# A channel MLP's head: three token tiles transposed raw and multiplied in cells of 386 columns, instead of two in cells of 258

## The chip, the cores and the metric

One core of one Trainium2 chip. The metric is the device time of one execution in microseconds; 398.56 us is the median of three runs of the kernel before (398.45 to 398.8).

## The reference

```python
def _gelu(x):
    return jax.nn.gelu(x, approximate=True)

def _layernorm(x, axis=-1, eps=1e-5):
    m = jnp.mean(x, axis=axis, keepdims=True)
    v = jnp.var(x, axis=axis, keepdims=True)
    return (x - m) / jnp.sqrt(v + eps)

def reference(x, w1, b1, w2, b2):
    y = _layernorm(x, axis=-1)
    h = _gelu(jnp.einsum("bsd,df->bsf", y, w1) + b1)
    return jnp.einsum("bsf,fd->bsd", h, w2) + b2
```

x is 1 x 2048 x 1024, w1 1024 x 3584, w2 3584 x 1024, all bf16; x and the biases are normal times 0.05.

## The kernel before, in words

**Tiling.** The 2048 tokens are 16 tiles of 128, four tiles to a block of 512 columns. D = 1024 is eight depth tiles, F = 3584 is 28 rows of 128. For each block the first product fills 28 PSUM rows of 512 columns (`pe_row`, line 386: eight matmuls of 512 columns, one for each depth tile), ScalarE puts each through Gelu with b1 into `hT_sb` (`act_gelu`, line 409), and the second product (`out_chunk`, line 451) makes eight groups of 28 matmuls from `hT_sb` and w2. VectorE adds b2 and SP stores. Both products want the tokens on the free axis, so x is transposed into `yT_sb`. For blocks 1 to 3 VectorE does the layernorm and the transposes (lines 255 to 269 and 312) under TensorE's work. PE works through one list in a fixed order; each engine has such a list, and they meet in semaphores.

**The head.** Block 0 can't wait for all of that. SP's queue loads x tile 0, x tile 1, four w1 chunks, x tile 2, four more chunks, x tile 3 (`SP_FIRST_LOADS`), then the wide w1 chunks, block 1, w2, b2 and the rest. A chunk of the first eight is two depth tiles of 512 columns: 256 KB in rows of 1 KB. PE runs 27 spin matmuls (`warm`), then transposes tiles 0 and 1 raw, not normalised (`pe_T`, line 342), into four PSUM banks; ScalarE copies them to `yT_sb` (line 358). Then comes the wave: seven rows (`R`), one in each of seven PSUM banks. For each row and depth tile a cell of 258 columns (`pe_wave`, line 399) multiplies both raw tiles and two columns of ones; the ones give the sum over depth of w1, which a raw tile needs for its mean. Tile 2 is normalised by VectorE (`ops_norm`), transposed after cell 50, and multiplied in 56 cells of 128 columns; then tile 3 the same way, transposed at cell 36 of tile 2's pass. Both pass through the bank `ps_t`.

**Making up for raw.** The statistics of the raw tiles are turned into rows (`ops_row_turn`, line 484) and spread over the partitions by ScalarE (`put_row_spread`, line 490). For each of the seven rows VectorE then adds minus the mean times the column sum (line 518) and multiplies by the reciprocal deviation (line 521): the fix, before that row's Gelu. The 21 later rows of block 0 are full rows of 512 columns. For them the raw tiles are centred in place in `yT_sb` (`ops_centre`, line 511, one subtraction per tile, allowed when the raw cells are done), and only the multiplication by the reciprocal deviation is left (line 425).

**Order around it.** VectorE's list in the head is: statistics of tiles 0 and 1, b1's transposes (line 496) and its cast (line 499), the turn, statistics and normalisation of tiles 2 and 3, centring, seven fixes. After it `crit` (scalings, b2 additions) and `fill` (layernorm and transposes of the next block) are merged by estimated due times, from `T_PE_START`, `T_DVE_START`, `est` and the cost that each entry carries. `new_unit` deals out PSUM banks: the seven of the wave, then the five of `ps_1` in a ring; a row waits for the Gelu that last read its bank. `SLOT_0` puts block 0's raw tiles at columns 128 to 383 of `yT_sb`, tile 2 at 384, tile 3 at 0.

Of the kernel before, what the change touches and what calls it, by code (L numbers as in the profile page):

```python
# [20 lines left out]
RAW = (0, 1)  # L21
# [5 lines left out]
ROWS = ((0, 1, 2, 3), (4, 5, 6))  # L27
QUARTERS = (0, 2, 4, 6, 8)
T2_AT = 50
T3_AT = 36  # L30
W1_EARLY = 2
W1_EARLY_COLS = 512
W1_COLS = (512, 1024, 1024)
N_W2_CHUNKS = 4
SP_FIRST_LOADS = ("x0", "x1", "w0", "w1", "w2", "w3", "x2", "w4", "w5", "w6", "w7", "x3")
ACT_FIRST_LOADS = ("b1",)
SLOT_0 = (1, 2, 3, 0)
N_ONES = 2

T_PE_START = 5.8  # L40
T_DVE_START = 21.0
# [54 lines left out]
def bass_standalone__mixer_channel_mlp__prompt_kernel(  # L96
# [25 lines left out]
    assert TPB == 4 and RAW == (0, 1) and sum(ROWS, ()) == tuple(range(R))  # L122

    w1_chunks = [(j0, j1, k * W1_EARLY_COLS, (k + 1) * W1_EARLY_COLS) for k in range(W1_EARLY)
                 for j0, j1 in zip(QUARTERS[:-1], QUARTERS[1:])]
# [21 lines left out]
    with ExitStack() as es:  # L147
# [6 lines left out]
        yT_sb = sb("yT_sb", [P, 2, DT, TB], BF16)  # L154
# [3 lines left out]
        b1r_sb = sb("b1r_sb", [32, P], BF16)  # L158
        b1t_sb = sb("b1t_sb", [P, 32], BF16)
# [3 lines left out]
        stat_r = sb("stat_r", [P, 2, 4], F32)  # L163
        row_r = sb("row_r", [P, 4, P], F32)
# [9 lines left out]
        ps_2 = ps("ps_2", [P, NB2, 512], F32)  # L174
        ps_1b = ps_1[:, :, :].bitcast(BF16)
# [39 lines left out]
        def issue(item):  # L215
            if item == "b1":
                dma(b1r_sb[0:FT, :], b1.rearrange("(t p) -> t p", p=P), "b1", F * 2, waits=["b1z"])
            elif item[0] == "x":
                load_x_tile(int(item[1:]))
            elif item[0] == "w" and int(item[1:]) < len(w1_chunks):  # L220
                load_w1(int(item[1:]))
# [22 lines left out]
        pool.op(lambda e: e.memset(b1r_sb[:, :], 0.0), sig="b1z")  # L244
        one0 = SLOT_0[0] * P - N_ONES
        pool.op(lambda e: e.memset(yT_sb[:, 0, :, one0:one0 + N_ONES], 1.0), sig="onecols")
# [54 lines left out]
        def ops_T(i):  # L301
            blk, t = divmod(i, TPB)
            waits = [y_ev[i][-1]]
            if blk - 2 in mm1_done:
                waits.append(mm1_done[blk - 2])
            res = []
            for tq in range(4):
                for q in range(4):
                    src = x_sb[32 * tq:32 * (tq + 1), i, :].rearrange("p (j q a) -> p j q a", j=DT, q=4)[:, :, q, :]
                    dst = yT_sb[32 * q:32 * (q + 1), blk % 2, :, t * P + 32 * tq:t * P + 32 * (tq + 1)]  # L310
                    lastop = (tq == 3 and q == 3)
                    res.append((lambda e, src=src, dst=dst: e.transpose(out=dst, in_=src),  # L312
                                waits, (f"tr{i}" if lastop else None), 0.47))
            yT_ev[i] = [f"tr{i}"] * DT
            return res
# [6 lines left out]
        bank_of = {"t": ps_t[:, 0, :], "2_0": ps_2b[:, 0, :], "2_1": ps_2b[:, 1, :], "1_4": ps_1b[:, 4, :]}  # L322
        slot = lambda i: SLOT_0[i] if i < TPB else i % TPB

        def pe_T(i, groups, banks):
            blk = i // TPB
            t = slot(i)
# [21 lines left out]
            for k, (g0, g1) in enumerate(zip(groups[:-1], groups[1:])):  # L349
                bname = banks[k]  # L350
                if bname != prev:
                    off = 0
                prev = bname
                done = max(m for m in range(len(banks)) if banks[m] == bname)
                src = bank_of[bname][:, off:off + (g1 - g0) * P].bitcast(I32)
                src = src.rearrange("p (j s) -> p j s", j=g1 - g0)
                dst = yT_sb[:, blk % 2, g0:g1, t * P:(t + 1) * P].bitcast(I32)
                act.op(lambda e, dst=dst, src=src: e.copy(out=dst, in_=src), waits=[f"tp{i}_{done}"],  # L358
                       sig=f"te{i}_{k}")
                off += (g1 - g0) * P  # L360
                bank_read[bname] = f"te{i}_{k}"
# [5 lines left out]

        def new_unit():
            u = unit_n[0]
            unit_n[0] += 1  # L370
            bank = first_ring[u] if u < len(first_ring) else ("1", (u - len(first_ring)) % NB1)
            waits = [bank_gelu[bank]] if bank in bank_gelu else []
            name = f"{bank[0]}_{bank[1]}"
            if not waits and name in bank_read:
                waits.append(bank_read[name])
            return bank, waits

        def unit_bank(bank):
            return (ps_1 if bank[0] == "1" else ps_2)[:, bank[1], :]

        def pe_row(b, r, bank, waits, sig):
            for dt in range(DT):
                w = list(waits) if dt == 0 else []
                w += [f"w1c{w1_chunk_of(r, dt)}"]
                w += [yT_ev[b * TPB + t][dt] for t in range(TPB)]
                pe.op(lambda e, b=b, r=r, dt=dt, bank=bank: e.matmul(  # L386
                    unit_bank(bank)[:, 0:TB], lhsT=w1_sb[:, dt, r * P:(r + 1) * P], rhs=yT_sb[:, b % 2, dt, :],
                    start=(dt == 0), stop=(dt == DT - 1)),
                    waits=w, sig=(sig if dt == DT - 1 else None))
            pe_t[0] += DT * _mm_us(TB)  # L390
            est[sig] = pe_t[0]

        def pe_wave(r, dt, tiles, bank, waits, sig):
            n0 = slot(tiles[0]) * P - (N_ONES if tiles[0] == 0 else 0)
            n1 = (slot(tiles[-1]) + 1) * P
            w = list(waits) + [f"w1c{w1_chunk_of(r, dt)}"] + [yT_ev[t][dt] for t in tiles]
            if tiles[0] == 0:
                w.append("onecols")
            pe.op(lambda e: e.matmul(  # L399
                unit_bank(bank)[:, n0:n1], lhsT=w1_sb[:, dt, r * P:(r + 1) * P], rhs=yT_sb[:, 0, dt, n0:n1],  # L400
                start=(dt == 0 and tiles[0] in (0, 3)), stop=(dt == DT - 1), skip_group_check=True),
# [15 lines left out]
        def mm1_row(b, r):  # L417
# [4 lines left out]
            if b == 0:  # L422
                reg = raw_cols(bank)
                ready = f"sc_{r}"
                crit.append((est[sig], (lambda e, reg=reg: e.tensor_tensor(out=reg, in0=reg, in1=row_b(1), op=ALU.mult),  # L425
                                        [sig, "row_r"], ready, 0.45), 0))
# [10 lines left out]
        def out_chunk(b, st, c0, c1, region, prev_store):  # L437
# [11 lines left out]
            for ft in range(FT):  # L449
                sl = slot(b * TPB + st)  # L450
# [28 lines left out]
        def ops_row_turn():  # L479
            res = []  # L480
            for tq in range(4):
                src = flat[32 * tq:32 * (tq + 1), :, :].to_broadcast([32, 4, 32])
                dst = row_r[0:32, :, 32 * tq:32 * (tq + 1)]
                res.append((lambda e, src=src, dst=dst: e.transpose(out=dst, in_=src), ["rstd0", "rstd1"],  # L484
                            ("row_q" if tq == 3 else None), 0.31))
# [7 lines left out]
        def ops_b1():  # L493
            res = []
            for q in range(4):
                res.append((lambda e, q=q: e.transpose(out=b1t_sb[32 * q:32 * (q + 1), :],
                                                       in_=b1r_sb[:, 32 * q:32 * (q + 1)]),
                            ["b1", "b1z"], ("b1t" if q == 3 else None), 0.2))
            res.append((lambda e: e.tensor_copy(out=b1_sb[:, :], in_=b1t_sb[:, 0:FT]), ["b1t"], "b1c", 0.18))
            return res  # L500

        row_b = lambda k: row_r[:, :, :].rearrange("p (t k) s -> p t k s", k=2)[:, :, k, :]
        raw_cols = lambda bank: unit_bank(bank)[:, slot(0) * P:(slot(1) + 1) * P].rearrange("p (t s) -> p t s", t=2)
        bank_col = lambda bank: bank[1] + (0 if bank[0] == "1" else NB1)

        def ops_centre():
            res = []
            for t in RAW:
                xt = yT_sb[:, 0, :, slot(t) * P:(slot(t) + 1) * P]
                m = row_r[:, 2 * t, :].unsqueeze(1).to_broadcast([P, DT, P])  # L510
                res.append((lambda e, xt=xt, m=m: e.tensor_tensor(out=xt, in0=xt, in1=m, op=ALU.subtract),  # L511
                            ["row_r", "wave01"], f"ctr{t}", 1.23))
# [23 lines left out]
        pe_T(1, GROUPS_0, ("2_1", "1_4"))  # L536
        put_row_spread()
# [9 lines left out]
        cells = [(r, dt) for rows in ROWS for j0, j1 in zip(QUARTERS[:-1], QUARTERS[1:])  # L547
                 for r in rows for dt in range(j0, j1)]
        for n, (r, dt) in enumerate(cells):
            if n == T2_AT:  # L550
                pe_T(2, GROUPS_1, ("t",))
            wave_cell(r, dt, RAW, "wave01" if n == len(cells) - 1 else None)
        n = 0
        for j0, j1 in zip(HALVES[:-1], HALVES[1:]):
            for r in range(R):
                for dt in range(j0, j1):
                    if n == T3_AT:
                        pe_T(3, GROUPS_1, ("t",))
                    n += 1
                    wave_cell(r, dt, (2,), f"w2_{r}" if dt == DT - 1 else None)  # L560
        cs_ev = {}
        for c0, c1, src in ((0, NB1, ps_1[:, 0:NB1, one0:one0 + 1]), (NB1, R, ps_2[:, 0:NB2, one0:one0 + 1])):
            mine = [r for r in range(R) if c0 <= bank_col(wave[r][0]) < c1]
            act.op(lambda e, c0=c0, c1=c1, src=src: e.mul(ncs[:, c0:c1].unsqueeze(2), src, -1.0),
                   waits=[f"w2_{mine[-1]}"], sig=f"cs{c0}")
            for r in mine:
                cs_ev[r] = f"cs{c0}"
        for r in range(R):
# [3 lines left out]
            for o in ops_fix(r, wave[r][0]):  # L572
# [3 lines left out]
        for t in RAW:  # L576
            yT_ev[t] = [f"ctr{t}"] * DT
# [93 lines left out]
```

## Time and profile before

| | |
|---|---|
| median of three runs | 398.56 us |
| the profiled execution | 398.81 us |
| its span | 397.6 us |
| PE busy | 391.5 us (98%) |
| full rows, line 386: one matmul | 379 ns, 821 recorded |
| second product, line 451: one matmul | 379 ns (128 x 512), 964 recorded with the narrow ones |
| PE, waits for w1 in the head (matmul rows) | 1.4 us |
| VectorE, DVE transposes, line 312 | 83.7 us, 192 of them |
| w1 chunks of 256 KB: from issue to landing | 5.5 us (median of 8) |

A matmul's duration holds the depth of the array, so it is longer than the distance from one to the next; its end is modelled. Some matmul records are missing. "PEld" is the loading of weights, "SPq" SP's issuing of DMAs; a bracket gives the idle time of the engine before the group and what ended it. Idle time of an engine that is not on the path costs nothing.

### The profile page before, as it was taken

The numbers are of one execution on the slowest core, as the hardware profiler recorded it, in microseconds if no ns is written. First come the engines' busy times: TensorE is split into PE (matmuls) and PEld (weight loads), VectorE is DVE, ScalarE is ACT, GpSimd is POOL, SyncE is SP. The second block draws the span as 40 slices with busy tenths as digits, with TensorE's granted clock in tenths as the row PEclk, the third lists the DMA queues.
The fourth block names the chain that finished last, engine by engine and source line by source line (L and its number), as shares of the span: only waits on it lengthen the run. The fifth ranks groups of instructions, "written<-read, shape, count | busy, mean of one in ns | idle before, by whom it ended". The sixth has DMA issues, their size and how long they took to land.

```text
span 397.6 us, 4718 instructions
## 1 busy us (share of the span) xinstructions
PE 391.5 (98%) x2015; PEld 189.7 (48%) x2050; DVE 154.3 (39%) x335; ACT 82.7 (21%) x124; POOL 10.6 (3%) x56
## 2 busy tenths in 40 slices
PE   8999999999999999999999999999999999999998
PEld 7844444444444444444444444444444444444446
DVE  5759898989999005988100000001100000001111
ACT  3264430000134432000024433100003334400000
POOL 2101000020001000000000000000000000000000
DMA  7999930000000000000000000000000000000001
GB/s 252 375 387 387 387 145 15 26 26 16 26 1 2 0 0 2 26 14 28 26 15 0 0 2 0 12 16 26 13 28 13 2 0 0 2 13 26 15 26 28
DMA packets 16350, 23.64 MB, mean 59 GB/s; under 512 B 1482, under 2 KB 8522, under 8 KB 16330
## 3 DMA queue, kind: packets, MB, share of 16 engines
q1 hardware_dynamic: 16288, 23.33, 16.7%
q8 instruction: 16, 0.26, 0.3%
q14 instruction: 4, 0.03, 0.0%
q10 hardware_dynamic: 42, 0.01, 0.0%
HBM read 19.14 MB, written 4.19 MB: 59 GB/s over the span
## 4 chain that ended last, share of the span: by engine, by line
PE 95%; DMA 2%; SPq 1%; issue 1%; DVE 1%; POOL 0%
PE ps L451 48%; PE ps L386 45%; DMA x_sb<-in_x_dram 2%; SPq L192 1%; PE ps L399 1%; DVE st_sb L255 0%; PE ps_t L342 0%; POOL rstd_sb L262 0%; DVE x_sb L269 0%; DVE o_sb L462 0%; DVE mv_sb L265 0%
## 5 line engine op out<-in xcount | busy, mean ns | idle before, releaser
L451 PE MATMUL ps<-w_sb,hT_sb 128*128 128x512 bf16 (+1 forms) x964 | 193.4, 360 | 0.8
L386 PE MATMUL ps<-yT_sb,w_sb 128*128 128x512 bf16 x821 | 180.8, 379 | 1.0
L451 PEld LDWEIGHTS ps<-w_sb,hT_sb 128*128 128x128 bf16 x980 | 91.3, 98 | 102.6
L409 ACT ACTIVATE hT_sb<-ps,b_sb 128x512 bf16<-128x512 f32 x112 | 76.8, 688 | 253.2 <-PE ps L386 231.8
L386 PEld LDWEIGHTS ps<-yT_sb,w_sb 128*128 128x128 bf16 x840 | 82.1, 98 | 98.9
L462 DVE TENSOR_TENSOR o_sb<-ps,b_sb 128x512 bf16<-128x512 f32 (+1 forms) x35 | 22.6, 646 | 198.9 <-PE ps L451 198.9
L312 DVE STREAM_TRANSPOSE yT_sb<-x_sb 32x256 bf16<-32x256 bf16 x192 | 83.7, 436 | 26.4 <-PE ps L386 23.3
L255 DVE BATCH_NORM_STATS2 st_sb<-x_sb 128x6 f32<-128x512 bf16 x32 | 20.9, 671 | 7.3 <-DMA x_sb<-in_x_dram 7.3
L399 PE MATMUL ps<-yT_sb,w_sb 128*128 128x128 bf16 (+1 forms) x168 | 13.4, 237 | 1.4 <-DMA w_sb<-in_w_dram 1.4
L399 PEld LDWEIGHTS ps<-yT_sb,w_sb 128*128 128x128 bf16 x168 | 11.4, 98 | 3.1 <-DMA w_sb<-in_w_dram 2.2
L262 POOL TENSOR_TENSOR rstd_sb<-mv_sb,nhalf 128x1 f32<-128x1 f32 x14 | 7.7, 549 | 115.0 <-DVE mv_sb L265 115.0
L425 DVE TENSOR_TENSOR ps<-ps,row_r 128x256 f32<-128x256 f32 x21 | 8.9, 427 | 4.7 <-PE ps L386 4.7
L269 DVE TENSOR_SCALAR x_sb<-x_sb,mv_sb,rstd_sb 128x1024 bf16<-128x1024 bf16 x14 | 7.6, 544 | 3.3 <-POOL rstd_sb L262 2.7
L473 PE MATMUL ps<-const-bfloat16-1.0 128*128 128x128 bf16 x30 | 3.4, 300 | 0.8 <-PEq L656 0.8
L473 PEld LDWEIGHTS ps<-const-bfloat16-1.0 128*128 128x128 bf16 x30 | 3.0, 139 | 0.8 <-issue 0.8
L518 DVE SCALAR_TENSOR_TENSOR ps<-row_r,ncs,ps 128x256 f32<-128x256 f32 x7 | 3.4, 480 | 0.0
L265 DVE BATCH_NORM_AGGREGATE mv_sb<-st_sb 128x2 f32<-128x15 f32 x14 | 3.1, 222 | 0.4
L358 ACT COPY yT_sb<-ps_t 128x512 int32<-128x512 int32 (+1 forms) x3 | 1.5, 516 | 7.7 <-PE ps_t L342 7.7
L521 DVE TENSOR_TENSOR ps<-ps,row_r 128x256 f32<-128x256 f32 x7 | 3.0, 432 | 0.2
L490 ACT COPY row_r<-row_r 32x512 f32<-32x512 f32 x3 | 1.9, 617 | 3.2 <-DVE row_r L484 3.2
L511 DVE TENSOR_TENSOR yT_sb<-yT_sb,row_r 128x1024 bf16<-128x1024 bf16 x2 | 2.4, 1216 | 0.0
L342 PE MATMUL ps_t<-ident,x_sb 128*128 128x128 bf16 x20 | 1.7, 226 | 0.1
(21 smaller groups left out, 12.5 us busy)
## 6 DMA issues: line engine op xcount, KB each, us to landing
w_sb<-in_w_dram SPq DMA_DIRECT2D x4, 1792.0 KB, 18.3
w_sb<-in_w_dram SPq DMA_DIRECT2D x2, 2048.0 KB, 15.9
out_dram<-o_sb SPq DMA_DIRECT2D x31, 128.0 KB, 1.7
x_sb<-in_x_dram SPq DMA_DIRECT2D x3, 1024.0 KB, 14.3
w_sb<-in_w_dram SPq DMA_DIRECT2D x8, 256.0 KB, 5.5
x_sb<-in_x_dram SPq DMA_DIRECT2D x4, 256.0 KB, 4.2
w_sb<-in_w_dram SPq DMA_DIRECT2D x1, 1024.0 KB, 9.0
b_sb<-in_b_dram SPq DMA_DIRECT2D x1, 256.0 KB, 14.3
```

The source lines that it names most:

```text
L192: dma_q[0].op(lambda e, dst=dst, src=src: e.dma_start(dst, src), waits=waits, sig=sig, sem="d_" + sig, inc=16)
L255: return (lambda e, i=i, h=h, pw=pw: e.bn_stats(st_sb[i][:, 6 * h:6 * (h + 1)], x_sb[:, i, h * pw:(h + 1) * pw]), [x_ev[i][h if len(x_ev[i ...
L262: pool.op(lambda e, i=i, dst=dst, mv=mv: e.tensor_tensor(out=dst, in0=mv[:, 1:2], in1=nhalf[:, i:i + 1], op=ALU.pow), waits=[f"mv{i}", "nh ...
L269: return (lambda e, i=i, c0=c0, c1=c1: e.tensor_scalar(out=x_sb[:, i, c0:c1], in0=x_sb[:, i, c0:c1], scalar1=mv_sb[:, i, 0:1], scalar2=rst ...
L312: res.append((lambda e, src=src, dst=dst: e.transpose(out=dst, in_=src), waits, (f"tr{i}" if lastop else None), 0.47))
L386: pe.op(lambda e, b=b, r=r, dt=dt, bank=bank: e.matmul(unit_bank(bank)[:, 0:TB], lhsT=w1_sb[:, dt, r * P:(r + 1) * P], rhs=yT_sb[:, b % 2, ...
L399: pe.op(lambda e: e.matmul(unit_bank(bank)[:, n0:n1], lhsT=w1_sb[:, dt, r * P:(r + 1) * P], rhs=yT_sb[:, 0, dt, n0:n1], start=(dt == 0 and ...
L409: act.op(lambda e, r=r, n0=n0, n1=n1, bank=bank: e.activation(out=hT_sb[:, r, n0:n1], in_=unit_bank(bank)[:, n0:n1], func=ACT.Gelu_apprx_tanh,
L425: crit.append((est[sig], (lambda e, reg=reg: e.tensor_tensor(out=reg, in0=reg, in1=row_b(1), op=ALU.mult), [sig, "row_r"], ready, 0.45), 0))
L451: pe.op(lambda e, sl=sl, ft=ft, c0=c0, c1=c1, bank=bank: e.matmul(ps_2[:, bank, 0:c1 - c0], lhsT=hT_sb[:, ft, sl * P:(sl + 1) * P], rhs=w2 ...
L462: crit.append((est[sig], (lambda e, ob=ob, c0=c0, c1=c1, bank=bank: e.tensor_tensor(out=o_sb[:, ob, c0:c1], in0=ps_2[:, bank, 0:c1 - c0], ...
L473: pe.op(lambda e: e.matmul(ps_1[:, 0, 0:P], lhsT=ones, rhs=ones, start=True, stop=True))
```

## The change

It loads tile 2 third and transposes it raw like tiles 0 and 1, so that a cell has 386 columns (three tiles and the two columns of ones) and the pass for tile 2 is gone; only tile 3 is normalised first and has a pass of 56 cells, transposed at cell 42 of the raw cells. The first eight w1 chunks are four depth tiles of 256 columns (rows of 512 bytes), and the cells go by pairs of rows. b1 is transposed on PE into `ps_t`, between tiles 1 and 2, and copied by ScalarE; its zero fill and VectorE's five instructions for it go. `yT_sb` has two columns more: the ones are at 0 and 1, every tile starts two columns later, and full rows read from column 2. In the first seven rows the raw tiles stand at columns 128 to 511 of the bank and tile 3 at 0; in the later rows tiles stand in order, so `out_chunk` picks its columns of `hT_sb` by row. Turn and spread carry six rows, the fixes and scalings 384 columns. Centring is four subtractions, each over two depth tiles of three token tiles, two before row 0's fix and two behind it. The transposes' bank joins the ring of PSUM banks, ahead of the five of `ps_1`.

```diff
--- before.py
+++ after.py
...
-RAW = (0, 1)
+RAW = (0, 1, 2)
...
-ROWS = ((0, 1, 2, 3), (4, 5, 6))
-QUARTERS = (0, 2, 4, 6, 8)
-T2_AT = 50
-T3_AT = 36
-W1_EARLY = 2
-W1_EARLY_COLS = 512
+ROWS = ((0, 1), (2, 3), (4, 5), (6,))
+CENTRE = (0, 2, 4, 6, 8)
+T3_AT = 42
+W1_EARLY = 4
+W1_EARLY_COLS = 256
...
-SP_FIRST_LOADS = ("x0", "x1", "w0", "w1", "w2", "w3", "x2", "w4", "w5", "w6", "w7", "x3")
+SP_FIRST_LOADS = ("x0", "x1", "x2", "w0", "w1", "w2", "w3", "x3", "w4", "w5", "w6", "w7")
...
-SLOT_0 = (1, 2, 3, 0)
...
-T_PE_START = 5.8
-T_DVE_START = 21.0
+T_PE_START = 5.0
+T_DVE_START = 27.0
...
-                 for j0, j1 in zip(QUARTERS[:-1], QUARTERS[1:])]
+                 for j0, j1 in zip(HALVES[:-1], HALVES[1:])]
...
-        yT_sb = sb("yT_sb", [P, 2, DT, TB], BF16)
+        yT_sb = sb("yT_sb", [P, 2, DT, N_ONES + TB], BF16)
...
-        b1r_sb = sb("b1r_sb", [32, P], BF16)
-        b1t_sb = sb("b1t_sb", [P, 32], BF16)
+        b1r_sb = sb("b1r_sb", [FT, P], BF16)
...
-        stat_r = sb("stat_r", [P, 2, 4], F32)
-        row_r = sb("row_r", [P, 4, P], F32)
+        stat_r = sb("stat_r", [P, len(RAW), 4], F32)
+        row_r = sb("row_r", [P, 2 * len(RAW), P], F32)
...
         def issue(item):
...
-                dma(b1r_sb[0:FT, :], b1.rearrange("(t p) -> t p", p=P), "b1", F * 2, waits=["b1z"])
+                dma(b1r_sb[:, :], b1.rearrange("(t p) -> t p", p=P), "b1", F * 2)
...
-        pool.op(lambda e: e.memset(b1r_sb[:, :], 0.0), sig="b1z")
-        one0 = SLOT_0[0] * P - N_ONES
-        pool.op(lambda e: e.memset(yT_sb[:, 0, :, one0:one0 + N_ONES], 1.0), sig="onecols")
+        pool.op(lambda e: e.memset(yT_sb[:, 0, :, 0:N_ONES], 1.0), sig="onecols")
...
-        bank_of = {"t": ps_t[:, 0, :], "2_0": ps_2b[:, 0, :], "2_1": ps_2b[:, 1, :], "1_4": ps_1b[:, 4, :]}
-        slot = lambda i: SLOT_0[i] if i < TPB else i % TPB
+        bank_of = {"t": ps_t[:, 0, :], "2_0": ps_2b[:, 0, :], "2_1": ps_2b[:, 1, :], "1_2": ps_1b[:, 2, :], "1_3": ps_1b[:, 3, :],
+                   "1_4": ps_1b[:, 4, :]}
+        ycol = lambda i: N_ONES + (i % TPB) * P
+        raw_at = TB - len(RAW) * P
+        one0 = raw_at - N_ONES
...
         def pe_T(i, groups, banks):
...
-            t = slot(i)
...
+        ring = [("t", 0)] + [("1", k) for k in range(NB1)]
+
         def new_unit():
...
-            bank = first_ring[u] if u < len(first_ring) else ("1", (u - len(first_ring)) % NB1)
+            bank = first_ring[u] if u < len(first_ring) else ring[(u - len(first_ring)) % len(ring)]
...
-            name = f"{bank[0]}_{bank[1]}"
+            name = "t" if bank[0] == "t" else f"{bank[0]}_{bank[1]}"
...
         def unit_bank(bank):
-            return (ps_1 if bank[0] == "1" else ps_2)[:, bank[1], :]
+            return ps_tf if bank[0] == "t" else (ps_1 if bank[0] == "1" else ps_2)[:, bank[1], :]
...
         def pe_row(b, r, bank, waits, sig):
...
-                    unit_bank(bank)[:, 0:TB], lhsT=w1_sb[:, dt, r * P:(r + 1) * P], rhs=yT_sb[:, b % 2, dt, :],
+                    unit_bank(bank)[:, 0:TB], lhsT=w1_sb[:, dt, r * P:(r + 1) * P], rhs=yT_sb[:, b % 2, dt, ycol(0):ycol(0) + TB],
...
         def pe_wave(r, dt, tiles, bank, waits, sig):
-            n0 = slot(tiles[0]) * P - (N_ONES if tiles[0] == 0 else 0)
-            n1 = (slot(tiles[-1]) + 1) * P
+            raw = tiles == RAW
+            n0, n1 = (one0, TB) if raw else (0, raw_at)
+            y0 = 0 if raw else ycol(tiles[0])
...
-            if tiles[0] == 0:
+            if raw:
...
-                unit_bank(bank)[:, n0:n1], lhsT=w1_sb[:, dt, r * P:(r + 1) * P], rhs=yT_sb[:, 0, dt, n0:n1],
-                start=(dt == 0 and tiles[0] in (0, 3)), stop=(dt == DT - 1), skip_group_check=True),
+                unit_bank(bank)[:, n0:n1], lhsT=w1_sb[:, dt, r * P:(r + 1) * P], rhs=yT_sb[:, 0, dt, y0:y0 + n1 - n0],
+                start=(dt == 0), stop=(dt == DT - 1), skip_group_check=True),
...
-                reg = raw_cols(bank)
+                reg = raw_cols(bank, 0)
...
-                                        [sig, "row_r"], ready, 0.45), 0))
+                                        [sig, "row_r"], ready, 0.57), 0))
...
-                sl = slot(b * TPB + st)
+                sl = (st + raw_at // P) % TPB if b == 0 and ft < R else st
...
         def ops_row_turn():
...
-                src = flat[32 * tq:32 * (tq + 1), :, :].to_broadcast([32, 4, 32])
+                src = flat[32 * tq:32 * (tq + 1), :, :].to_broadcast([32, 2 * len(RAW), 32])
...
-                res.append((lambda e, src=src, dst=dst: e.transpose(out=dst, in_=src), ["rstd0", "rstd1"],
-                            ("row_q" if tq == 3 else None), 0.31))
+                res.append((lambda e, src=src, dst=dst: e.transpose(out=dst, in_=src), [f"rstd{t}" for t in RAW],
+                            ("row_q" if tq == 3 else None), 0.38))
...
         def put_row_spread():
...
-        def ops_b1():
-            res = []
-            for q in range(4):
-                res.append((lambda e, q=q: e.transpose(out=b1t_sb[32 * q:32 * (q + 1), :],
-                                                       in_=b1r_sb[:, 32 * q:32 * (q + 1)]),
-                            ["b1", "b1z"], ("b1t" if q == 3 else None), 0.2))
-            res.append((lambda e: e.tensor_copy(out=b1_sb[:, :], in_=b1t_sb[:, 0:FT]), ["b1t"], "b1c", 0.18))
-            return res
+        def pe_b1():
+            pe.op(lambda e: e.transpose(out=ps_t[:, 0, 0:FT], in_=b1r_sb[:, :], identity=ident[0:FT, 0:FT]),
+                  waits=["ident", "b1", bank_read["t"]], sig="b1t")
+
+        def put_b1():
+            act.op(lambda e: e.copy(out=b1_sb[:, :], in_=ps_t[:, 0, 0:FT]), waits=["b1t"], sig="b1c")
+            bank_read["t"] = "b1c"
...
-        raw_cols = lambda bank: unit_bank(bank)[:, slot(0) * P:(slot(1) + 1) * P].rearrange("p (t s) -> p t s", t=2)
+        raw_cols = lambda bank, c0: unit_bank(bank)[:, c0:c0 + len(RAW) * P].rearrange("p (t s) -> p t s", t=len(RAW))
...
         def ops_centre():
...
-            for t in RAW:
-                xt = yT_sb[:, 0, :, slot(t) * P:(slot(t) + 1) * P]
-                m = row_r[:, 2 * t, :].unsqueeze(1).to_broadcast([P, DT, P])
+            for k, (j0, j1) in enumerate(zip(CENTRE[:-1], CENTRE[1:])):
+                xt = yT_sb[:, 0, j0:j1, ycol(RAW[0]):ycol(RAW[0]) + len(RAW) * P]
+                xt = xt.rearrange("p j (t s) -> p j t s", t=len(RAW))
+                m = row_b(0).unsqueeze(1).to_broadcast([P, j1 - j0, len(RAW), P])
...
-                            ["row_r", "wave01"], f"ctr{t}", 1.23))
+                            ["row_r", f"raw_{R - 1}"], f"ctr{k}", 0.83))
...
         def ops_fix(r, bank):
...
-            reg = raw_cols(bank)
+            reg = raw_cols(bank, raw_at)
...
-        nm = {i: ops_norm(i) for i in (2, 3)}
+        nm = {3: ops_norm(3)}
...
-        seq = st[0][:2] + st[1][:2] + [st[0][2], st[1][2]] + ops_b1() + turn
-        for i in (2, 3):
-            seq += st[i] + nm[i]
-        seq += ctr
+        seq = st[0] + st[1] + st[2] + turn + st[3] + nm[3] + ctr[:2]
...
+        pe_b1()
+        pe_T(2, GROUPS_0, ("1_3", "1_2"))
+        put_b1()
...
-        cells = [(r, dt) for rows in ROWS for j0, j1 in zip(QUARTERS[:-1], QUARTERS[1:])
+        cells = [(r, dt) for rows in ROWS for j0, j1 in zip(HALVES[:-1], HALVES[1:])
...
-            if n == T2_AT:
-                pe_T(2, GROUPS_1, ("t",))
-            wave_cell(r, dt, RAW, "wave01" if n == len(cells) - 1 else None)
-        n = 0
-        for j0, j1 in zip(HALVES[:-1], HALVES[1:]):
-            for r in range(R):
-                for dt in range(j0, j1):
-                    if n == T3_AT:
-                        pe_T(3, GROUPS_1, ("t",))
-                    n += 1
-                    wave_cell(r, dt, (2,), f"w2_{r}" if dt == DT - 1 else None)
+            if n == T3_AT:
+                pe_T(3, GROUPS_1, ("t",))
+            wave_cell(r, dt, RAW, f"raw_{r}" if dt == DT - 1 else None)
...
-                   waits=[f"w2_{mine[-1]}"], sig=f"cs{c0}")
+                   waits=[f"raw_{mine[-1]}"], sig=f"cs{c0}")
...
-            for o in ops_fix(r, wave[r][0]):
+            for o in ops_fix(r, wave[r][0]) + (ctr[2:] if r == 0 else []):
...
-            yT_ev[t] = [f"ctr{t}"] * DT
+            yT_ev[t] = [f"ctr{k}" for k, (j0, j1) in enumerate(zip(CENTRE[:-1], CENTRE[1:])) for _ in range(j0, j1)]
...
```

More of the change, by code (lines that the diff above doesn't have):

```diff
@@ L121, in bass_standalone__mixer_channel_mlp__prompt_kernel @@
     assert all(c[-1] == DT for c in (GROUPS_0, GROUPS_1, HALVES))
-    assert TPB == 4 and RAW == (0, 1) and sum(ROWS, ()) == tuple(range(R))
+    assert TPB == 4 and RAW == (0, 1, 2) and sum(ROWS, ()) == tuple(range(R))
     w1_chunks = [(j0, j1, k * W1_EARLY_COLS, (k + 1) * W1_EARLY_COLS) for k in range(W1_EARLY)
-                 for j0, j1 in zip(QUARTERS[:-1], QUARTERS[1:])]
+                 for j0, j1 in zip(HALVES[:-1], HALVES[1:])]
     c0 = W1_EARLY * W1_EARLY_COLS
@@ L174, in bass_standalone__mixer_channel_mlp__prompt_kernel @@
         ps_2 = ps("ps_2", [P, NB2, 512], F32)
+        ps_tf = ps_t[:, 0, :].bitcast(F32)
         ps_1b = ps_1[:, :, :].bitcast(BF16)
@@ L309, in ops_T @@
                     src = x_sb[32 * tq:32 * (tq + 1), i, :].rearrange("p (j q a) -> p j q a", j=DT, q=4)[:, :, q, :]
-                    dst = yT_sb[32 * q:32 * (q + 1), blk % 2, :, t * P + 32 * tq:t * P + 32 * (tq + 1)]
+                    dst = yT_sb[32 * q:32 * (q + 1), blk % 2, :, ycol(i) + 32 * tq:ycol(i) + 32 * (tq + 1)]
                     lastop = (tq == 3 and q == 3)
@@ L356, in pe_T @@
                 src = src.rearrange("p (j s) -> p j s", j=g1 - g0)
-                dst = yT_sb[:, blk % 2, g0:g1, t * P:(t + 1) * P].bitcast(I32)
+                dst = yT_sb[:, blk % 2, g0:g1, ycol(i):ycol(i) + P].bitcast(I32)
                 act.op(lambda e, dst=dst, src=src: e.copy(out=dst, in_=src), waits=[f"tp{i}_{done}"],
```

## The prediction

> **What bounds the kernel now.** I read the page's engine totals and chain of waits first, then the time line of PE and the windows of the head, then the groups by form. The chain belongs to PE almost from end to end:
>
> ```profile
> PE 391.5 (98%) x2015; PEld 189.7 (48%) x2050; DVE 154.3 (39%) x335; ACT 82.7 (21%) x124; POOL 10.6 (3%) x56
> PE 95%; DMA 2%; SPq 1%; issue 1%; DVE 1%; POOL 0%
> ```
>
> So only what moves PE's first full row (line 386, row 7) moves the end: from there PE runs without a gap (49 matmuls in 10.74 us, over and over in the chain). The head of PE's time line (start, length, group):
>
> ```profile
> 4.75 0.34 PE L473 MATMUL ps<-const-bfloat16-1.0 128*128 128x128 bf16 x3
> 6.21 3.69 PE L399 MATMUL ps<-yT_sb,w_sb 128*128 128x258 bf16 x32 [1.13 <-DMA w_sb<-in_w_dram]
> 10.16 2.34 PE L399 MATMUL ps<-yT_sb,w_sb 128*128 128x258 bf16 x18 [0.26 <-DMA w_sb<-in_w_dram]
> 12.34 0.61 PE L342 MATMUL ps_t<-ident,x_sb 128*128 128x128 bf16 x8
> 12.79 3.02 PE L399 MATMUL ps<-yT_sb,w_sb 128*128 128x258 bf16 x42
> 15.90 0.62 PE L342 MATMUL ps_t<-ident,x_sb 128*128 128x128 bf16 x8
> 16.36 4.41 PE L399 MATMUL ps<-yT_sb,w_sb 128*128 128x128 bf16 x76
> ```
>
> Durations there hold a pipeline's depth, so I take pitches from start to start. A group of 76 narrow matmuls lasts 4.41 with a last one of 0.219: (4.41-0.219)/75 = 0.0559. Sixteen cells of 258 columns lasted 1.92 with a last one of 0.274: 0.1098. A full row's matmul: (10.74-0.379)/48 = 0.2158. All three are columns x 0.4167 ns plus about 2.4 ns, so a cell of 386 columns has a pitch of 0.1633. The last group begins at 16.36 and hands over after 76 x 0.0559, so row 7 begins at 20.61 now.
>
> From 6.21 to 20.61 are 14.40 us. The work in it is 56 x 0.1098 + 112 x 0.0559 + 16 transposes x 0.0559 = 13.30. So **1.10 us of it are waits**: for w1 chunks, and for tiles 2 and 3. The weight loads show them:
>
> ```profile
> 10.16 0.55 PEld L399 LDWEIGHTS ps<-yT_sb,w_sb 128*128 128x128 bf16 x6 [0.54 <-DMA w_sb<-in_w_dram]
> 10.91 0.55 PEld L399 LDWEIGHTS ps<-yT_sb,w_sb 128*128 128x128 bf16 x6 [0.20 <-DMA w_sb<-in_w_dram]
> 11.67 0.55 PEld L399 LDWEIGHTS ps<-yT_sb,w_sb 128*128 128x128 bf16 x6 [0.20 <-DMA w_sb<-in_w_dram]
> 13.62 2.01 PEld L399 LDWEIGHTS ps<-yT_sb,w_sb 128*128 128x128 bf16 x36 [0.30 <-ACT yT_sb L358]
> ```
>
> They also date the landings: w0 (third transfer in SP's queue) at 6.20, x2 (seventh; VectorE's wait ends) at 9.01, w4, w5, w6 at 10.16, 10.91, 11.67, x3 (twelfth) at 13.06. A 256 KB transfer lands every (9.01-6.20)/4 = 0.70 to 0.75 us.
>
> **The start moves back.** x2 takes the third place in the queue and w0 the fourth, so w0 lands at about 6.20 + 0.70 = 6.90. Bounds: x0 landed at 3.42, so x2 cannot be there before 3.42 + 2 x 0.70 = 4.82, nor w0 before 5.52; above, SP handed out 3584 rows (four tiles of 128, eight chunks of 256, one of 1024) between 0.8 and 7.7 us, so a chunk of 512 rows takes 0.99 at most: 7.19. Tile 2 must be transposed by then too: four transposes end 0.39 after x2 (3 x 0.056 + 0.219), ScalarE's copy of 256 takes 0.37, hand-overs some 0.09: x2 + 0.85, that is 5.7 to 7.05; its second half is due four cells later. The three spin matmuls and the transpose of b1 stand before the first cell and are covered by the same wait; b1 had landed by 6.07, where VectorE took it without a wait. I take **6.90 for the first cell, 0.69 later than now**.
>
> The chunks change shape too, 512 bytes per row and not 1 KB. Rates from the windows: with 1 KB rows in flight the DMA moved 369 and 373 GB/s (11 to 12 us), with 2 KB rows 385 to 388 later; halving a row cost some 4%. A chunk now feeds 8 cells x 0.1633 = 1.31 us of PE, against 0.70 to 0.99 us to land, so no later chunk is waited for.
>
> The Trainium skill, "DMA: Bandwidth & Descriptors", section "Why small descriptors are slow (HBM only)", speaks against this: each packet costs about 3 cycles beside one per 32 bytes. By it 1 KB as two packets takes 38 cycles and not 35, a chunk 0.76 and not 0.70, and the first cell would be 0.06 later; the traces' 4% for the step above is of the same order.
>
> **The work shrinks.** 56 x 0.1633 + 8 transposes x 0.0559 + 56 x 0.0559 = 9.14 + 0.45 + 3.13 = 12.72. That is 0.58 less: 56 matmuls fewer at 2.4 ns, and the eight transposes of tile 2 move into the wait ahead.
>
> **Waits that go.** All 1.10 us, if tile 3 is ready at its place, cell 42: 6.90 + 42 x 0.1633 = 13.76. x3 is eighth now, so it lands about 10.2 (w4's row); VectorE is then free (three tiles' statistics at 1.24 plus 0.17 each behind x0's 3.42, and x2's, end by 7.7; POOL's power 0.55; four turns of 192 columns at 0.300 + 64 x 1.04 ns = 0.37 give 9.9). From landing to transposes took 13.06 to 15.90 = 2.84; so 13.0, with 0.7 us to spare. ScalarE does three spreads of 0.617 + 256 x 0.836 ns = 0.83 by 12.4, before tile 3's copy needs it.
>
> **A wait that comes.** Centring is four subtractions of 768 elements, two of them behind row 0's fix, and row 7 needs them. None of this shape is in the trace; the nearest rows are:
>
> ```profile
> L462 DVE TENSOR_TENSOR o_sb<-ps,b_sb 128x512 bf16<-128x512 f32 x31 | 21.4, 692 | 194.2 <-PE ps L451 194.2
> L462 DVE TENSOR_TENSOR o_sb<-ps,b_sb 128x128 bf16<-128x128 f32 x4 | 1.2, 292 | 4.7 <-PE ps L451 4.7
> L518 DVE SCALAR_TENSOR_TENSOR ps<-row_r,ncs,ps 128x256 f32<-128x256 f32 x7 | 3.4, 480 | 0.0
> L521 DVE TENSOR_TENSOR ps<-ps,row_r 128x256 f32<-128x256 f32 x7 | 3.0, 432 | 0.2
> L511 DVE TENSOR_TENSOR yT_sb<-yT_sb,row_r 128x1024 bf16<-128x1024 bf16 x2 | 2.4, 1216 | 0.0
> ```
>
> The first two give 400/384 = 1.04 ns an element. A subtraction is then 1216 - 256 x 1.04 = 950 ns, with the next starting 0.08 before its end (1.13 apart for two of 1.216 now), so 0.87 apart. Call T the moment when the raw cells end. VectorE starts at T + 0.20 (the last cell drains); two subtractions to T + 1.94; fix 0 takes 0.51 + 0.13 from its first half to its second and 0.34 + 0.13 on to the next instruction (256 columns grow to 384): T + 3.05; the third subtraction ends at T + 4.00, the fourth at T + 4.87. PE spends 56 x 0.0559 = 3.13 on tile 3, reaches row 7's depth tile 4 at T + 3.99 and would reach tile 6 at T + 4.43. It waits until about T + 4.92: **0.5 us lost in row 7**. Bounds: 0.3 if an operation costs only 0.9 of this, 1.55 if each still costs 1.216.
>
> **What costs nothing.** Row 7 takes the transposes' bank, free since tile 3's copy, so it does not wait for a Gelu. Row 8 needs Gelu 0 by T + 5.4 and has it at T + 3.9; row 9 needs Gelu 1 by T + 7.1: fix 1 ends T + 6.0, Gelu (0.688) T + 6.8. From there a fix pair costs 0.85 + 0.27 = 1.12 against 1.73 a row. The 21 scalings of 384 columns (0.427 + 0.133 = 0.56) have that cover too; without it they would cost 21 x 0.13 = 2.8 us. VectorE ended block 1's transposes at 79 us, and they are due at 105. The bigger chunks and w2 keep their places in bytes; row 8 needs its chunk 5 us after it lands. The rows of yT now begin 4 bytes off: cells that begin 252 bytes off already run at columns x 0.4167 + 2.4 ns, so I price this at 0 (bound: 0.1 ns x 840, under 0.1 us).
>
> **The sum.** +0.69 (start) - 0.58 (work) - 1.10 (waits) + 0.50 (row 7) = -0.49 us. T is 6.90 + 9.59 = 16.49. The profiled execution took 398.81 (span 397.6 and 1.2 around it), 0.25 above the median of 398.56; I subtract from the median: 398.56 - 0.49 = **398.1 us**.
>
> **Rivals.**
>
> *The first cell starts earlier* (chance 0.25). At 3.5 to 4.5 us, when w0 follows x1, the DMA moved only 159 and 213 GB/s. If x2's long rows fill that hole, w0 lands near 6.3 and x2 near 5.5, so tile 2's copy allows 6.35. That is 0.55 better: 397.5. Against it: the hole may be latency of the first transfers whatever they are.
>
> *Centring is the bound* (0.15). Subtractions that still cost 1.216 apiece make row 7 wait 1.55, and 0.49 becomes -0.56: 399.1. Against it is the slope of 1.04 ns an element; for it, that the new operand runs over three tiles with a stride.
>
> *TensorE's clock falls back* (0.11), the slower side. Early in the kernel the pitch was 0.106 (nine spin matmuls in 1.16, the last 0.311) until about 3.9 us, 3.1 us after the first; then it halved. Now a 1.13 us gap follows and the fast pitch holds. After the change PE is nearly idle from 4.8 to 6.9, with eight transposes and three spin matmuls inside. If that is long enough to lose the fast pitch, the cells run at 0.32 for some 3.1 us and lose 1.55: -0.49 + 1.55 = +1.06, 399.6. It decides as soon as the gap counts as idle.
>
> The Trainium skill, "TensorE: Matmul & The Clock Gate", section "What's actually happening", puts the fall at one whole idle window of about 3.4 us, and by that this rival does not come; its Part 4 says that transposes do not count as busy in the same way, which speaks for it. No row here has a gap of that length.
>
> *512-byte rows move at half rate* (0.09). Then a chunk takes 1.40, more than the 1.31 of its cells, and w4 to w7 come at 13.2, 14.6, 16.0, 17.4 with x3 at 11.8; the raw cells end at 18.06 and not 16.49: +1.08, 399.6. Against it: the 4% above.
>
> That the change doesn't remove its waits (tile 3 late at cell 42) would need x3 after 10.9, and is part of the last rival.
>
> **How the numbers follow.** The likeliest, 0.40, is the sum, with its own range 397.7 to 398.6. What this measurement can tell from no change is 0.2%, 0.8 us: faster is below 397.76, slower above 399.36. Faster is the early start with a little of the main case's edge, 0.27; slower the clock and the half rate, 0.20; the rest, 0.53. The range holds the main case, the early start and the centring rival: 397.2 to 399.4.
>
> **What would show it.** In the changed profile: first 386-column cell near 6.9 (right between 6.6 and 7.2); no DMA wait inside the 56 cells; their pitch 0.163; no wait ahead of tile 3's transposes; the subtractions at 950 ns; a gap of about 0.5 us between row 7's depth tiles 5 and 6, credited to VectorE's subtraction; row 8 beginning near 21.9 and not 22.3. A pitch of 0.32, a wait on w1 after the first chunk, or a first cell outside 6.4 to 7.3 would prove it wrong.

## The result, and the profile after

The changed kernel takes 399.38 us (median of 20 runs, 399.04 to 399.75), the kernel before, measured beside it, 398.64 (20 runs, 397.99 to 399.4): ratio 1.0018, 95% interval 1.0011 to 1.0025. It is slower by about 0.7 us; the forecast was faster by 0.5. The profiled execution took 399.20 us, span 397.8.

The head does nearly what the working said. PE's time line of the kernel after (start, length, engine, line, group):

```profile
5.52 0.62 PE L340 MATMUL ps<-ident,x_sb 128*128 128x128 bf16 x8 [0.26 <-DMA x_sb<-in_x_dram]
5.97 0.33 PE L474 MATMUL ps<-const-bfloat16-1.0 128*128 128x128 bf16 x3
6.58 7.02 PE L400 MATMUL ps<-yT_sb,w_sb 128*128 128x386 bf16 x42 [0.27 <-DMA w_sb<-in_w_dram]
13.44 0.61 PE L340 MATMUL ps_t<-ident,x_sb 128*128 128x128 bf16 x8
13.88 5.58 PE L400 MATMUL ps<-yT_sb,w_sb 128*128 128x386 bf16 x70
19.52 1.41 PE L386 MATMUL ps_t<-yT_sb,w_sb 128*128 128x512 bf16 x5
21.19 0.60 PE L386 MATMUL ps_t<-yT_sb,w_sb 128*128 128x512 bf16 x2 [0.26 <-DVE yT_sb L512]
21.63 8.84 PE L386 MATMUL ps<-yT_sb,w_sb 128*128 128x512 bf16 x40
```

The first cell begins at 6.58, the 42 cells run at (7.02 - 0.327)/41 = 0.163 (the last one alone lasts 0.327), tile 3's transposes follow without a gap, the raw cells end at 13.88 + 14 x 0.1633 = 16.17, and row 8 begins at 21.63, against 20.61 + 1.73 = 22.34 in the profile of before. So this execution was 0.7 us **ahead** of that one at row 8. The loss must lie behind it. The chain of waits over block 1 of the kernel after (start, length; the first line begins block 1's first product, the last its second product; rows in the sixth bank stand as ps_t):

```profile
104.86 1.74 PE ps L386 x8
106.60 0.05 issue
106.65 3.42 PE ps L386 x15
110.07 1.74 PE ps_t L386 x8
111.80 5.64 PE ps L386 x26
...
151.72 1.74 PE ps_t L386 x8
153.46 6.69 PE ps L452 x31
```

The same two ends in the kernel before:

```profile
105.37 1.73 PE ps L386 x8
...
153.72 7.34 PE ps L451 x34
```

Block 1's first product runs from 104.86 to 153.46, 48.60 us; before, from 105.37 to 153.72, 48.35. It waits for no other engine, and the records of a row's eight matmuls give 1.74 and not 1.73. Blocks 2 and 3 take 48.61 and 48.59, while the second product takes 48.35 in both kernels. A quarter of a microsecond is lost in each block, spread over its rows: 0.25/224 = 1.1 ns in each matmul in the mean, and 840 of them make 0.9 to 1.0 us.

### The profile page after: what moved, and what is told of

Same layout as the page of the kernel before. It is cut to its first block, busy times and chain, and to the rows that moved or that the text cites. A ratio compares the mean times of both kernels' runs of the same rounds, so it can differ in the third digit from the quotient of the medians.

```text
span 397.8 us, 4607 instructions
## 1 busy us (share of the span) xinstructions
PE 392.4 (99%) x1960; PEld 186.3 (47%) x1995; DVE 159.3 (40%) x331; ACT 82.9 (21%) x126; POOL 10.5 (3%) x55
## 4 chain that ended last, share of the span: by engine, by line
PE 96%; DMA 1%; DVE 1%; issue 1%; SPq 0%; DVEq 0%
PE ps L452 48%; PE ps L386 38%; PE ps_t L386 7%; PE ps L400 2%; DMA w_sb<-in_w_dram 1%; DVE yT_sb L512 1%; SPq L190 0%; DVE ps L522 0%; DVE ps L519 0%; PE ps_t L340 0%; DVE o_sb L463 0%; DVEq L81 0%
## 5 line engine op out<-in xcount | busy, mean ns | idle before, releaser
L386 PE MATMUL ps<-yT_sb,w_sb 128*128 128x512 bf16 x683 | 153.4, 379 | 0.7
L410 ACT ACTIVATE hT_sb<-ps,b_sb 128x512 bf16<-128x512 f32 x94 | 64.1, 688 | 237.7 <-PE ps L386 217.8
L386 PEld LDWEIGHTS ps<-yT_sb,w_sb 128*128 128x128 bf16 x696 | 67.6, 97 | 83.4
L386 PE MATMUL ps_t<-yT_sb,w_sb 128*128 128x512 bf16 x138 | 34.0, 379 | 0.6 <-DVE yT_sb L512 0.3
L386 PEld LDWEIGHTS ps_t<-yT_sb,w_sb 128*128 128x128 bf16 x144 | 13.8, 97 | 17.8 <-DVE yT_sb L512 1.2
L410 ACT ACTIVATE hT_sb<-ps_t,b_sb 128x512 bf16<-128x512 f32 x18 | 12.4, 687 | 17.6 <-PE ps_t L386 14.7
L400 PE MATMUL ps<-yT_sb,w_sb 128*128 128x386 bf16 (+1 forms) x112 | 12.6, 272 | 0.3 <-DMA w_sb<-in_w_dram 0.3
L426 DVE TENSOR_TENSOR ps<-ps,row_r 128x384 f32<-128x384 f32 x17 | 9.3, 564 | 3.5 <-PE ps L386 3.3
L400 PEld LDWEIGHTS ps<-yT_sb,w_sb 128*128 128x128 bf16 x112 | 8.5, 97 | 4.0 <-DMA w_sb<-in_w_dram 0.4
L512 DVE TENSOR_TENSOR yT_sb<-yT_sb,row_r 128x768 bf16<-128x768 bf16 x4 | 3.6, 951 | 3.4 <-PE ps L400 3.4
L519 DVE SCALAR_TENSOR_TENSOR ps<-row_r,ncs,ps 128x384 f32<-128x384 f32 x7 | 4.3, 612 | 0.0
L522 DVE TENSOR_TENSOR ps<-ps,row_r 128x384 f32<-128x384 f32 x7 | 4.0, 566 | 0.2
```

The costliest lines, as they stand in the source:

```text
L386: pe.op(lambda e, b=b, r=r, dt=dt, bank=bank: e.matmul(unit_bank(bank)[:, 0:TB], lhsT=w1_sb[:, dt, r * P:(r + 1) * P], rhs=yT_sb[:, b % 2, ...
L400: pe.op(lambda e: e.matmul(unit_bank(bank)[:, n0:n1], lhsT=w1_sb[:, dt, r * P:(r + 1) * P], rhs=yT_sb[:, 0, dt, y0:y0 + n1 - n0], start=(d ...
L410: act.op(lambda e, r=r, n0=n0, n1=n1, bank=bank: e.activation(out=hT_sb[:, r, n0:n1], in_=unit_bank(bank)[:, n0:n1], func=ACT.Gelu_apprx_tanh,
```

## The experiments

**1 to 4: what stretches the full rows.** Three things changed for a full row: it begins 4 bytes into its row of `yT_sb`; the rows are 1028 bytes apart and not 1024; and it may stand in the sixth bank. Two kernels give the changed kernel other columns, two give the kernel before other rows:

```diff
 x1_rows_on_64 (after), x4_rows_on_16: Y_AT = 8, Y_ROW = 520
+Y_AT = 32
+Y_ROW = 544
...
-        yT_sb = sb("yT_sb", [P, 2, DT, N_ONES + TB], BF16)
+        yT_sb = sb("yT_sb", [P, 2, DT, Y_ROW], BF16)
...
-        ycol = lambda i: N_ONES + (i % TPB) * P
+        ycol = lambda i: Y_AT + (i % TPB) * P
...
 x2_before_rows_1028 (before): Y_AT = 0, Y_ROW = 514; x3_before_start_4: Y_AT = 2, Y_ROW = 544
-        yT_sb = sb("yT_sb", [P, 2, DT, TB], BF16)
+        yT_mem = sb("yT_mem", [P, 2, DT, Y_ROW], BF16)
+        yT_sb = yT_mem[:, :, :, Y_AT:Y_AT + TB]
```

> The changed kernel with thirty more columns in yT_sb: tiles start 64 bytes into a row and rows are 1088 bytes apart, so that every read of a full row begins on a multiple of 64 bytes. Theory A (a full row's read that begins off a boundary costs 1.2 ns a matmul, 840 matmuls, 1.0 us): the first product of blocks 1 to 3 takes 48.35 us each and not 48.60, and the time falls by 0.9 to 1.0, to about 398.4. Theory B (the sixth bank in the ring, or VectorE's traffic, stretches the rows): 48.60 stays, 399.4.

> The kernel before, with two unused columns behind each row of yT_sb: rows 1028 bytes apart, so that depth tiles begin 0, 4, 8, 12 bytes off a multiple of 16. Theory A: 48.60 us a block and about 399.6 (+0.95). Theory B: 48.35 and 398.6, since ring, engines and waits are those of before.

> The kernel before, rows of yT_sb 1088 bytes apart and every read beginning 4 bytes into its row. Theory A with the start as the cause: every matmul pays, 48.6 to 49.1 us a block. If it is the odd distance of rows and not the start: 48.35. Theory B: 48.35.

> The changed kernel with tiles 16 bytes into a row and rows 1040 bytes apart: every read begins on a multiple of 16 bytes, few on 32 or 64. Theory A with a grid of 16 bytes: 48.35 us a block. With a grid of 32 or 64: half or more of the matmuls pay, 48.45 to 48.6. Theory B: 48.60.

x1 takes 398.62 us (12 runs), 0.9996 of before (0.9987 to 1.0004). x2 takes 399.34 (10 runs), 1.002 (1.001 to 1.003). One run each: x3 398.8, x4 398.38. The chain of x2, the kernel before with two unused columns behind each row (start, length, line, matmuls):

```profile
105.11 48.60 PE ps L389 x224
153.71 48.34 PE ps L454 x224
202.05 48.61 PE ps L389 x224
250.66 48.35 PE ps L454 x224
299.01 48.60 PE ps L389 x224
```

and of x3, where every read begins 4 bytes off but rows are 1088 bytes apart:

```profile
105.02 48.35 PE ps L389 x224
153.36 48.35 PE ps L454 x224
201.71 48.35 PE ps L389 x224
250.06 48.35 PE ps L454 x224
298.40 48.35 PE ps L389 x224
```

Line 389 is the first product, 454 the second. The two unused columns alone make the kernel before as slow as the changed one; the start of 4 bytes costs nothing; the changed kernel with rows of 1088 or 1040 bytes is back at 48.35 a block, with its six banks kept (x1, x4). So it is **the distance of the rows**, and theory B falls. Block 3, which begins at 299 us, shows the loss too, long after VectorE's last write to `yT_sb` (188 us), so it is in the reading.

**5: how fine the grid is.** Rows of 1032 bytes, `Y_ROW = 516`, in the kernel before:

> The kernel before with rows of yT_sb 1032 bytes apart, so that the reads begin 0 and 8 bytes off a multiple of 16 in turn. If any change of phase from one read to the next costs, a block's first product takes more than 48.35 us, up to 48.60; if only steps of 4 bytes do, 48.35.

The first product stayed at 48.35 us a block (215.83 ns from one matmul to the next). The run took 399.01 us, but its rows don't account for that: its span is 397.4, shorter than the 397.6 of the first profile of before, as its row 7 begins a little sooner (16.21 + 76 x 0.0559 = 20.46 against 20.61). So 1024, 1032, 1040 and 1088 bytes are free and 1028 is not. In x2 the distance from one matmul to the next is 217.0 ns in the mean, but not the same for all: by the matmul records of blocks 1 to 3 the next one starts some 214.5, 215.4, 219.5 and 218.6 ns after a depth tile whose row begins 0, 4, 8 and 12 bytes off a multiple of 16 (counted from the start of the tile). Cells of 386 columns, read over rows 1028 bytes apart, kept 0.163. What in the reading costs this stays open.

**6: the head of before, once more.** x1 has the head of the change and its rows in order, and it is still no faster than before. So the kernel before, unchanged, was profiled again:

> The kernel before, unchanged, profiled once more: how much of its head belongs to one execution. If the 1.10 us of waits and the first cell at 6.21 are its rule, row 7 begins at 20.6 again; the heads of the two kernels before with longer rows say 20.15 to 20.25, with the first cell at 5.96 to 6.07.

```profile
4.08 1.49 PE L342 MATMUL ps<-ident,x_sb 128*128 128x128 bf16 x12
5.97 6.08 PE L399 MATMUL ps<-yT_sb,w_sb 128*128 128x258 bf16 x50
11.88 0.61 PE L342 MATMUL ps_t<-ident,x_sb 128*128 128x128 bf16 x8
12.33 3.02 PE L399 MATMUL ps<-yT_sb,w_sb 128*128 128x258 bf16 x42
15.22 0.62 PE L342 MATMUL ps_t<-ident,x_sb 128*128 128x128 bf16 x8
15.68 4.41 PE L399 MATMUL ps<-yT_sb,w_sb 128*128 128x128 bf16 x76
```

Here 50 cells run without a wait for w1, where the first profile has three of them, 0.62 us together, and row 7 begins at 15.68 + 76 x 0.0559 = 19.93, 0.68 earlier than in the first profile. Row 8 is then at 21.65, where the changed kernel has 21.63 and x1 21.73. From 5.97 to 19.93 are 13.96 us for 13.30 of work: 0.66 on top of the work and not 1.10, and a start 0.24 earlier.

Nor is this 0.66 all waiting. The 50 cells last 6.08; at 0.110 apart, the last one 0.28 long, they would last 5.67. By the records each of the first five is followed only after 0.13 to 0.22, and from 6.93 on the distance is 0.110: the slow pace makes 0.4. Tile 2 is waited for 0.19, tile 3 0.04. x2, x3 and s1 have the head of before but for the distance of the rows, which gives five profiles of it: row 7 begins at 19.93, 20.15, 20.25, 20.46 and 20.61, w1 is waited for between 0 and 0.7 us, and two of the five (b2 and x2) begin their cells at the slow pace. So both the waits for w1 and the pace of the first cells belong to single executions, and the profile that the forecast was read from was the latest of the five.

**7: the wait that came.** In x1, ScalarE copies the means once to bf16 and the subtractions read those:

```diff
...
+            act.op(lambda e: e.copy(out=mean_b[:, :, :], in_=row_b(0)), waits=["row_r"], sig="mean_b")
...
-                m = row_b(0).unsqueeze(1).to_broadcast([P, j1 - j0, len(RAW), P])
+                m = mean_b[:, :, :].unsqueeze(1).to_broadcast([P, j1 - j0, len(RAW), P])
```

> The kernel with rows on 64 bytes, and the centring's means copied once to bf16 by ScalarE (one copy of 128 x 384 behind the spread), so that the subtractions have only 2-byte operands. Theory A (row 7's wait is VectorE's four subtractions and one fix in a line): if 2-byte operands shorten a subtraction from 0.95 us, at 0.55 each the last ends 1.6 us earlier, the two gaps of row 7 go, row 8 begins 0.55 to 0.6 us earlier, and the time falls to about 398.05. If they stay at 0.95: no change. Theory B (the gaps are hidden by something behind them, such as a later Gelu that row 9 waits for): the gaps go and come back in row 8 or 9, 398.6.

397.89 us (11 runs) against 398.51 for the kernel before: 0.9985, interval 0.9974 to 0.9995. This version **beats both kernels**, the one before by 0.6 us. The gaps in the changed kernel, on the loading of weights for row 7:

```profile
19.25 0.59 PEld L386 LDWEIGHTS ps_t<-yT_sb,w_sb 128*128 128x128 bf16 x4
20.31 0.11 PEld L386 LDWEIGHTS ps_t<-yT_sb,w_sb 128*128 128x128 bf16 x2 [0.47 <-DVE yT_sb L512]
21.18 0.11 PEld L386 LDWEIGHTS ps_t<-yT_sb,w_sb 128*128 128x128 bf16 x2 [0.76 <-DVE yT_sb L512]
```

Ahead of depth tiles 4 and 6 PE waits for the third and the fourth subtraction. Weights are loaded ahead of their matmuls, so the matmuls themselves stand still for less than these gaps, 0.59 us together. The subtraction in the changed kernel by form:

```profile
L512 DVE TENSOR_TENSOR yT_sb<-yT_sb,row_r 128x768 bf16<-128x768 bf16 x4 | 3.6, 951 | 3.4 <-PE ps L400 3.4
```

and with bf16 means, with PE's time line behind it:

```profile
L516 DVE TENSOR_TENSOR yT_sb<-yT_sb,mean_b 128x768 bf16<-128x768 bf16 x4 | 2.0, 552 | 3.7 <-PE ps L403 3.7
```

```profile
14.12 5.58 PE L403 MATMUL ps<-yT_sb,w_sb 128*128 128x386 bf16 x70
19.54 1.89 PE L389 MATMUL ps_t<-yT_sb,w_sb 128*128 128x512 bf16 x8
21.26 8.80 PE L389 MATMUL ps<-yT_sb,w_sb 128*128 128x512 bf16 x40
```

951 ns became 552, row 7's eight matmuls run in 1.73 and rows 8 to 12 (40 matmuls) follow without a gap: the wait does not come back. Row 8 begins at 21.26 and not at 21.73 as in x1, though the first cell came 0.14 later here (6.82 against 6.68). The means then carry bf16's rounding.

**8: the sixth bank.**

```diff
-        ring = [("t", 0)] + [("1", k) for k in range(NB1)]
+        ring = [("1", k) for k in range(NB1)]
```

> The kernel with rows on 64 bytes, and the transposes' bank left out of the ring: row 7 waits for Gelu 0 and row 8 for Gelu 1. Theory A: row 7 starts at about 20.2 and not 19.4, has no wait for the subtractions, and row 8 starts about 23.0 (Gelu 1 ends there), row 9 1.73 later: 1.3 us more in all, 399.9. If the sixth bank is of no use: 398.6.

400.02 us in one run, as theory A has it (399.9). PE's time line:

```profile
20.50 1.90 PE L388 MATMUL ps<-yT_sb,w_sb 128*128 128x512 bf16 x8 [0.72 <-ACT hT_sb L412]
23.36 6.86 PE L388 MATMUL ps<-yT_sb,w_sb 128*128 128x512 bf16 x31 [0.96 <-ACT hT_sb L412]
```

Row 7 waits for Gelu 0, row 8 for Gelu 1. With fixes of 384 columns and centring between them, this kernel needs the sixth bank.

**9 and 10: the shape of the chunks, and b1.** x1 with two depth tiles of 512 columns again, and raw cells in the order of before; and that with bf16 means and b1's transpose behind tile 2's:

```diff
 h2_chunks_1KB (x1)
-ROWS = ((0, 1), (2, 3), (4, 5), (6,))
+ROWS = ((0, 1, 2, 3), (4, 5, 6))
+QUARTERS = (0, 2, 4, 6, 8)
-W1_EARLY = 4
-W1_EARLY_COLS = 256
+W1_EARLY = 2
+W1_EARLY_COLS = 512
 h5_bf16_1KB_b1_late, besides
-        pe_b1()
         pe_T(2, GROUPS_0, ("1_3", "1_2"))
+        pe_b1()
```

> The kernel with rows on 64 bytes, and the first eight w1 chunks again two depth tiles of 512 columns (rows of 1 KB), the raw cells in the order of before (rows 0 to 3, then 4 to 6, by two depth tiles). If rows of 512 bytes delay the first cell, it begins at 6.3 to 6.45 (tile 2's copy then decides) and not 6.6 to 6.7, and the DMA moves 370 to 400 GB/s at 9 to 12 us and not 290: 0.2 to 0.4 us less, 398.3. If they do not, 6.6 to 6.7 stays and 398.6.

> Rows on 64 bytes, means in bf16, w1 chunks with rows of 1 KB, and b1's transpose behind tile 2's instead of ahead of it. Against the version with bf16 means (397.9): if tile 2's copy decides the first cell, it starts 0.1 earlier, 397.8; if the wide rows deliver no sooner and PE was not held up by b1, 397.9.

h2 takes 398.6 us (10 runs), 1.0005 (0.9995 to 1.0014); h5 397.92 (12 runs), 0.9979 (0.9966 to 0.9992), not to be told from 397.89 (its first cell came at 6.94). The windows of the changed kernel and then of h2 (length, busy time by engine, clock, DMA share, GB/s), 9 to 12 us:

```profile
9.00:12.00 3.00, 3.00 (x21) 1.78 (x19) 2.71 (x7) 1.70 (x3) 0.10 (x1) 1.00 1.20 294
```

```profile
9.00:12.00 3.00, 3.00 (x20) 1.79 (x19) 2.73 (x7) 1.68 (x3) 0.08 (x1) 1.00 1.10 353
```

Rows of 512 bytes do move slower, 294 GB/s against 353 with 1 KB, and the DMA engines are no less busy (1.20 against 1.10). In this window the five profiles with 512 bytes have 294 to 299, the seven with 1 KB 353 to 376. But PE is busy for all 3.00 us in both: a chunk has 1.31 us to land. The first cell did not come sooner either, as h2's time line shows:

```profile
4.15 1.49 PE L343 MATMUL ps<-ident,x_sb 128*128 128x128 bf16 x12
5.70 0.89 PE L343 MATMUL ps<-ident,x_sb 128*128 128x128 bf16 x8
6.97 7.02 PE L403 MATMUL ps<-yT_sb,w_sb 128*128 128x386 bf16 x42 [0.21 <-ACT yT_sb L359]
```

It waits for ScalarE's copy of tile 2, and that copy came late because the transposes ran at half pace in that execution (1.49 us for 12, where the changed kernel took 1.01).

## Why the prediction was wrong

**The step that failed: the reads of `yT_sb`, priced at 0.** The prediction named the 4 bytes and drew its price from cells that begin 252 bytes into a row. That evidence was right about the start (x3: 48.35 us a block). But those cells lie in rows 1024 bytes apart, and the change also made the distance 1028; nothing in the trace of before shows a full row read at another distance. By the chains it is 3 x 0.25 in blocks 1 to 3 and 0.20 in block 0 (36.46 us for its 168 matmuls in x2, 36.26 in x3), 0.95 us; the medians give 399.38 - 398.62 = 0.76 (after against x1) and 399.34 - 398.64 = 0.70 (x2 against before), with an interval for x2 of 0.4 to 1.2.

**The second: 1.10 us of waits and the start at 6.21, read from one execution.** The second profile of the same kernel has 0.66 and 5.97, and of the 0.66 only 0.23 are waits. With these the sum of the head is +0.93 (6.90 against 5.97) - 0.58 - 0.66 + 0.50 = +0.19 and not -0.49; with the first cell (6.58) and the wait (0.59) of the changed kernel's profile it is +0.61 - 0.58 - 0.66 + 0.59 = -0.04. x1, the change without its distance of rows, stands at 0.9996, with an interval of -0.5 to +0.2 us: no gain of the head can be measured, and the 0.49 that was forecast is at the edge of what this leaves possible.

**Luck.** 399.38 still lies inside the range of 397.2 to 399.4. The range reached that far for the centring rival, which did not come; that the distance of the rows costs about as much is chance.

**What held.** The work of 12.72 us: 56 cells at 0.163, eight transposes, 56 narrow matmuls without a gap. No wait for a chunk after the first, nor for tile 3. The subtraction at 951 ns (forecast 950), the fix's halves at 612 and 566 (0.613 and 0.565), the scalings at 564 (0.56). Row 7's last pair of depth tiles starts at 16.17 + 5.02 (forecast 4.92), so the wait is 0.6 and not 0.5; VectorE began at T + 0.28 and not 0.20. With the sixth bank rows 8 and 9 did not wait for Gelus 0 and 1; without it (h3) these hold up rows 7 and 8.

**Sizes off.** The first cell at 6.58 where 6.90 was taken; in the other executions it came between 6.58 and 6.97, as w0 or tile 2's copy decides. 512-byte rows cost 17% of the rate (353 to 294 GB/s), more than the 4% read from the step above; it stayed hidden. By the Trainium skill, "DMA: Bandwidth & Descriptors", section "Why small descriptors are slow (HBM only)", which puts about 3 cycles on each packet, the prediction's estimate was 38 cycles and not 35, 9% more time for a chunk. The windows give 20% more (353/294).

**The rivals.** The early start came by half (6.58, where it had 6.35 and the sum 6.90) and was worth nothing by itself, since before starts earlier too. The centring rival did not come: 951 ns, not 1216, so the cost follows the elements. TensorE's pace did not fall back once it was up: 42 cells at 0.163 right behind a gap of half a microsecond. That agrees with the Trainium skill, "TensorE: Matmul & The Clock Gate", section "What's actually happening", which asks for a whole idle window of about 3.4 us; no run here has a gap that long. The half rate did not come: 294 GB/s against 353. The slower side came by a mechanism that was none of the rivals.

## What to carry to other kernels

When a tile that TensorE streams hundreds of times gets two extra columns, look at the distance of its rows: here 1028 bytes cost every 512-column read half a per cent all through the kernel, and 1024, 1032, 1040 and 1088 cost nothing (1032 is a multiple of 8, the other three of 16; other distances were not tried). When a change moves the start of a row, ask for its stride too, and say which of the two the evidence holds fixed. Waits for DMAs and the pace of the first matmuls vary from execution to execution in the head of this kernel: a gain under one microsecond read from a single profile's gaps is not yet a gain.

## What was not expected of the hardware

Row distance: 512-column reads cost 217.0 ns at 1028 bytes and 215.8 at 1024, 1032, 1040 and 1088, while reads of 386 columns cost 0.163 us at 1028 and at 1088. VectorE: a subtraction of 128 x 768 in SBUF with bf16 data took 951 ns with an f32 second operand and 552 with a bf16 one. TensorE: in some executions the first transposes still run at half pace (12 in 1.49 us), in others at the full one (0.94 to 1.02), though the 27 spin matmuls ahead of them begin at 0.82 us and stand 0.107 apart in both kinds (the first profile of before and the second). In the second the first five cells of 258 columns ran slow too, while the profile's clock column reads 1.00 in both. What sets the moment isn't shown here.
